# Gated mix of memory attention and a spectral filter: the wait that is planned to end last is written first

## The chip, the cores and the metric

The kernel runs on one core of one Trainium2 chip. The metric is the time on the device in microseconds; lower is better. The core has five instruction streams: TensorE (PE, with its weight loads shown apart as PEld), VectorE (DVE), ScalarE (ACT), GpSimd (POOL) and SyncE (SP), which here only issues transfers. The streams know of each other through semaphores alone: an instruction raises one when it has finished, a transfer raises one when it has landed, and another stream waits until the semaphore has reached a value.

## The reference

Two branches are computed from the same x (2048 tokens, 640 channels, bf16) and mixed by a gate per token:

```python
g = sigmoid((x * gate_w).sum(-1, keepdims=True))
a = A_ref(x, wq, wk, wv, wo, beta)      # attention in 4 segments of 512, 32 heads of 20
b = B_ref(x, w_r, w_i)                  # irfft2(rfft2(x) * (w_r + 1j * w_i))
return g * a + (1 - g) * b

# A_ref, segment s:
p = softmax(q k^T * 20**-0.5 + causal mask);  a_dot = p v
a_mem = phi(q) M / (phi(q) z + 1e-6)          # phi(t) = t + 1 if t > 0 else exp(t)
o = sigmoid(beta) * a_mem + (1 - sigmoid(beta)) * a_dot
M += phi(k)^T v;  z += sum of phi(k)          # memory for the next segment
# then o @ wo
```

## The kernel before

All the work is recorded first and emitted afterwards. `Kern.record` calls, segment by segment, the projections of q, k and v (`project`, `proj_tile`, `v_tile`), the reading of the memory (`mem_read`), attention (`attend`: `qk_unit` for the logits, exponentials on ACT at L1271, causal masks on POOL at L1292, and `pv_flipped` or `pv_group` for p v), and the memory update; after the first segment also the whole spectral branch (`fft`), which is written as matrix products with tables and lies between the attention work in time. `finish_tile` multiplies by wo, adds the spectral part and stores. Matmuls all pass through the helper `mms` (L520 and L522), copies out of PSUM through `copy_alts` (L531 on ACT, L533 on DVE), transfers through `dma` (L554 and L556). So those lines stand for many places; the tile names tell them apart.

`Sched` holds the operations. `op` notes what each reads and writes and from this on which earlier operations it depends. `schedule` takes a fixed order (`ORDER`, 2328 entries, each an operation and its engine), and plans a start and an end `t1` for each operation from listed durations and hop costs (`HOPS`). It also chooses PSUM banks and semaphores, which adds dependences: a bank must have been emptied, a transfer's semaphore must be free, and only so many bytes may be in flight.

`emit` writes the program in the planned order. For each operation it collects the semaphores and values to wait for. It leaves out those that the engine is known to have passed, directly or through what it has already waited for. What is left is `kept`, a list of (planned end, semaphore, value). It is sorted by the planned end, and one `wait_ge` is written for each (L292), just ahead of the operation.

An instruction can carry one wait. In the built program the wait that was written first is carried by the instruction itself. The others become separate EVENT_SEMAPHORE instructions of the same engine directly ahead of it, with up to two waits in each. The profile shows them at L292. For a matmul the carried wait is on its weight load. Of the 2328 operations, 933 have no wait that is kept, 1162 have one, and 233 have two or more: 196 have two and 37 from three to eight.

Of the kernel before, what the change touches and what calls it, by code (L numbers as in the profile page):

```python
# [49 lines left out]
class Sched:  # L50
# [204 lines left out]
    def emit(self, *last):  # L255

        nc = self.nc
        prog = {e: nc.alloc_semaphore(f"prog_{e}") for e in ("pe", "act", "dve", "pool")}
        dsem = [nc.alloc_semaphore(f"dma_{i}") for i in range(self.nsem)]
        dcnt = [0] * self.nsem  # L260
        count = {e: 0 for e in prog}
        known = {e: {} for e in self.eng}
        for o in self.order:
            o.need_inc = o.dma
        for o in self.order:
            for p in o.preds + o.dyn:
                if not (p.eng == "pe" and o.eng == "pe"):
                    p.need_inc = True
        stamps = {}
        for o in self.order:  # L270
            e = o.eng
            k = known[e]
            waits = {}
            for p in o.preds + o.dyn:
                if p.eng == "pe" and e == "pe":
                    continue
                key, val, vc = stamps[p.id]
                if k.get(key, 0) >= val:
                    continue
                if waits.get(key, (0, None))[0] < val:  # L280
                    waits[key] = (val, vc, p.t1)
            kept = []
            for key, (val, vc, t1) in sorted(waits.items(), key=lambda q: -len(q[1][1])):
                if k.get(key, 0) >= val:
                    continue
                kept.append((t1, dsem[key] if isinstance(key, int) else prog[key], val))
                for kk, vv in vc.items():
                    if k.get(kk, 0) < vv:
                        k[kk] = vv
                k[key] = val  # L290
            for t1, sem, val in sorted(kept, key=lambda q: q[0]):
                self.eng[e].wait_ge(sem, val)  # L292
            h = o.alts[e][0](self.eng[e])
            if o.dma:
                i = o.stamp
                dcnt[i] += 16
                h.then_inc(dsem[i], 16)
                stamps[o.id] = (i, dcnt[i], dict(k))
            elif o.need_inc:
                count[e] += 1  # L300
                h.then_inc(prog[e], 1)
                vc = dict(k)
                if e == "pe":
                    pass
                stamps[o.id] = (e, count[e], vc)
            else:
                stamps[o.id] = (e, count[e], {})
        ends = {}
        for o in sorted(self.order, key=lambda o: o.t1):
            if o.name in last:  # L310
                ends.pop(o.stamp, None)
                ends[o.stamp] = stamps[o.id][1]
        return [(dsem[i], v) for i, v in ends.items()]
# [1301 lines left out]
```

## Time and profile before

| | |
|---|---|
| median of 3 runs | 246.04 us (245.78 to 247.57) |
| profiled execution, first to last instruction | 242.6 us |
| around it (246.04 − 242.6; the profiled execution has no time of its own beside its span) | 3.4 us |
| PE busy | 227.0 us (94%), 4361 matmuls |
| DVE, ACT, POOL busy | 199.9, 200.5, 167.5 us |
| granted TensorE clock | 1.00 |
| HBM traffic | 147 GB/s over the span |

How to read it: the busy time of an engine counts its work, not its waiting; waits that are instructions of their own (EVENT_SEMAPHORE) are not busy time. The chain of waits follows the work that ended last back to the start: each piece is an engine's work, or "issue", time between what released an instruction and its start. A piece such as "DVEq L292" is VectorE's sequencer at a separate wait. "a <- b" in the view of waits means that engine a stood idle until b ended.

### The profile page before, as it was taken

To read this page: it belongs to the slowest core of one execution; us is meant where nothing else is said; L and a number is where in the kernel's file an instruction comes from. 1 tells how busy PE (TensorE), PEld (TensorE's weight loads), DVE (VectorE), ACT (ScalarE), POOL (GpSimd) and SP (SyncE) were. 2 spreads that over 40 slices of the span, in tenths; PEclk is the share of its full clock that TensorE was granted. 3 is DMA by queue.
4 is the path that set the end of the run, shared out by engine and by line. 5 is a ranking of instruction groups with operands and counts; after the bars stand their busy time and mean duration, and the time that the engine had idled before them with its cause. 6 is when DMAs were issued, how large, how long until landed. Compare 5 with 4: busy or idle time off the path is not lost.

```text
span 242.6 us, 10273 instructions
## 1 busy us (share of the span) xinstructions
PE 227.0 (94%) x4361; PEld 140.8 (58%) x4361; DVE 199.9 (82%) x478; ACT 200.5 (83%) x243; POOL 167.5 (69%) x298
## 2 busy tenths in 40 slices
PE   7899999999979999999799979999999999899994
PEld 2574666666546565454566545556545467566794
DVE  0199988899999997999997898998899996937474
ACT  2468989898989999899899889999999998688801
POOL 8243069457959946828787894986989687759730
PEclk9999999999999999999999999999999999999999
DMA  7999859995985875957735863543767779554223
GB/s 167 305 327 226 207 169 200 253 214 152 246 241 116 167 192 149 189 161 217 192 99 172 199 187 111 178 113 112 212 179 171 199 143 244 109 88 84 87 63 108
DMA packets 58928, 42.17 MB, mean 174 GB/s; under 512 B 30020, under 2 KB 55172, under 8 KB 58884
## 3 DMA queue, kind: packets, MB, share of 16 engines
q1 hardware_dynamic: 57188, 40.71, 67.3%
q10 hardware_dynamic: 1696, 0.82, 1.2%
q8 instruction: 34, 0.56, 1.0%
q14 instruction: 10, 0.08, 0.1%
HBM read 23.32 MB, written 12.30 MB: 147 GB/s over the span
## 4 chain that ended last, share of the span: by engine, by line
PE 58%; DVE 17%; ACT 13%; DMA 4%; issue 2%; SPq 2%; POOL 2%; DVEq 0%; ACTq 0%; POOLq 0%
PE psum L522 53%; ACT ex L1271 10%; PE psum L520 5%; DVE G L1493 2%; DMA r<-r_scr 2%; DVE phk L1093 2%; DMA xsb<-in_A_x_dram 2%; DVE Pt L1447 2%; SPq L554 2%; DVE Yt L1452 2%; DVE oU L1534 1%; POOL ex L1292 1%; DVE xsb L914 1%; DVE xf L909 1%; DVE ub L533 1%
## 5 line engine op out<-in xcount | busy, mean ns | idle before, releaser
L1271 ACT ACTIVATE ex<-psum 128x2048 bf16<-128x2048 f32 (+4 forms) x92 | 138.5, 1506 | 13.2 <-PE psum L522 10.5
L1292 POOL TENSOR_SCALAR_AFFINE_SELECT ex<-ex 128x256 bf16<-128x256 bf16 (+2 forms) x224 | 123.2, 572 | 32.0 <-ACT ex L1271 27.9
L522 PE MATMUL psum<-qkp 20*64 20x64 bf16 (+5 forms) x1280 | 32.7, 270 | 3.3 <-ACT ex L1271 2.8
L522 PE MATMUL psum<-xT,wk 128*128 128x256 bf16 (+1 forms) x280 | 33.5, 273 | 1.2 <-DMA wk<-in_A_wk_dram 0.6
L522 PE MATMUL psum<-xT,wq 128*128 128x512 bf16 (+1 forms) x135 | 31.3, 380 | 0.0
L522 PE MATMUL psum<-wv,xT 128*32 128x320 bf16 (+3 forms) x400 | 29.5, 301 | 0.3 <-ACT gate L1121 0.2
L1447 DVE TENSOR_TENSOR Pt<-psum,Wt 128x642 bf16<-128x642 f32 x32 | 25.5, 821 | 0.8 <-PE psum L522 0.6
L522 PEld LDWEIGHTS psum<-qkp 20*64 20x64 bf16 x1280 | 13.5, 102 | 20.8 <-ACT ex L1271 14.2
L522 PEld LDWEIGHTS psum<-xT,wk 128*128 128x128 bf16 (+1 forms) x280 | 19.6, 97 | 9.2 <-DMA xT<-in_A_x_dram 1.3
L520 PE MATMUL psum<-wo,oU 128*32 128x320 bf16 x480 | 21.4, 300 | 0.7 <-DVE oU L1542 0.5
L522 PE MATMUL psum<-ex,va 128*32 128x64 bf16 (+3 forms) x576 | 17.6, 256 | 2.1 <-DVE dn L1160 1.3
L522 PEld LDWEIGHTS psum<-wv,xT 128*32 128x32 bf16 (+1 forms) x400 | 14.5, 96 | 7.7 <-issue 2.6
L522 PE MATMUL psum<-big,Ac 128*128 128x161 bf16 (+2 forms) x96 | 17.5, 257 | 1.6 <-DVE va L1123 1.4
L914 POOL TENSOR_TENSOR xsb<-xf 128x320 bf16<-128x320 bf16 (+2 forms) x9 | 7.6, 843 | 15.8 <-DVE xsb L914 11.7
L522 PE MATMUL psum<-big,Cp 128*128 128x321 bf16 (+1 forms) x96 | 17.8, 303 | 0.4
L1123 DVE TENSOR_TENSOR va<-psum,ebx 128x320 bf16<-128x320 f32 x32 | 15.3, 484 | 3.2 <-PE psum L522 2.2
L522 PEld LDWEIGHTS psum<-ex,va 128*32 128x32 bf16 x576 | 11.4, 96 | 10.8 <-POOL ex L1292 3.2
L1493 DVE TENSOR_TENSOR G<-eo,psum 128x320 bf16<-128x320 f32 x32 | 14.9, 479 | 2.4 <-PE psum L522 2.0
L533 DVE CAST ot<-psum 128x320 bf16<-128x320 f32 x18 | 8.4, 488 | 9.4 <-PE psum L520 7.4
L1080 ACT ACTIVATE et<-qu 128x512 bf16<-128x512 bf16 x25 | 15.3, 625 | 0.9 <-DVE phk L1093 0.9
L1452 POOL TENSOR_TENSOR Yt<-Pt 128x321 bf16<-128x321 bf16 x17 | 12.6, 748 | 4.9 <-PE psum L522 4.4
L522 PE MATMUL psum<-tt,Yt 128*128 128x256 bf16 (+1 forms) x96 | 15.6, 273 | 0.3 <-DVE mem L1165 0.2
(96 smaller groups left out, 399.5 us busy)
## 6 DMA issues: line engine op xcount, KB each, us to landing
qkp<-qk_scr SPq DMA_DIRECT2D x28, 160.0 KB
tt<-tab_tt SPq DMA_DIRECT2D x8, 512.0 KB, 4.1
qk_scr<-qu SPq DMA_DIRECT2D x12, 256.0 KB, 2.9
u_scr<-ub SPq DMA_DIRECT2D x12, 256.0 KB, 3.2
xsb<-in_A_x_dram SPq DMA_DIRECT2D x8, 320.0 KB, 5.5
oU<-u_scr SPq DMA_DIRECT2D x15, 128.0 KB, 3.0
out_dram<-ot SPq DMA_DIRECT2D x12, 160.0 KB
Wt<-in_B_w_r_dram SPq DMA_DIRECT2D x16, 80.2 KB, 3.1
```

The source lines that it names most:

```text
L520: h = e.matmul(dst, wt, r_, start=st, stop=sp_, **{**kw, "tile_position": (0, q), "skip_group_check": True})
L522: h = e.matmul(o_, l_, r_, start=st, stop=sp_, **kw)
L533: alts["dve"] = (lambda e: e.tensor_copy(dst(), src()), 67 + 1.04 * n, 68.0)
L554: return e.dma_start_transpose(d_, s_)
L914: self.either(lambda e, dst=dst, src=src, d0=d0, n=n, op=op: e.tensor_tensor(xs.ap(o + dst, [D, 2], [1, n]), xf.ap(src + d0, [321, 2], [1, ...
L1080: self.one("act", lambda e: e.activation(et.ap(0, [1, L]), qsl(), ACT.Exp), L, [qb], [b("et", pi_)], late, name="phi_exp")
L1123: self.one("dve", lambda e: e.tensor_tensor(va.ap(i * H * VW + h0 * VW, [VW, nh], [1, DH]), self.ps(bank, 0, [DH, nh], [1, DH]), self.ebx. ...
L1271: self.one("act", lambda e, d=d, q=q: e.activation(self.ex.ap(*d), self.ps(bank, *q), ACT.Exp, scale=SC), n, [bank], [self.exb(s, 2 * pr + ...
L1292: self.one("pool", lambda e: e.affine_select(self.ex.ap(e0 + d0, [1280, 4], [1, n], np_=np_), self.ex.ap(e0 + s0, [1280, 4], [1, n], np_=np_),
L1447: self.one("dve", lambda e, ri=ri, Pt=Pt, Wt=Wt, wo_=wo_, bank=bank: e.tensor_tensor(Pt.ap(ri * 322, [644, 2], [1, KD]), self.ps(bank, 0, ...
L1452: fn = lambda e, r=r, a0=a0, a1=a1, op=op, Pt=Pt, Yt=Yt: e.tensor_tensor(Yt.ap(r * 322, [1, KD]), Pt.ap(a0 * 322, [1, KD]), Pt.ap(a1 * 322 ...
L1493: self.one("dve", lambda e, q=q, n2=n2, bank=bank, eo=eo: e.tensor_tensor(self.G.ap(n2 * D + 639 * q, [1 - 2 * q, 320]), eo.ap(q, [1, 320] ...
```

## The change

One sort is turned round. The same waits on the same semaphores and values are written for each operation, but in falling order of the planned end. Operations with one wait or none are written as they were. By the build's rule above, for an operation with two waits the two change places: the one planned to end last is carried by the instruction, the other is the EVENT_SEMAPHORE. With more than two, the one planned to end last is carried, and the others share the EVENT_SEMAPHOREs.

```diff
-            for t1, sem, val in sorted(kept, key=lambda q: q[0]):
+            for t1, sem, val in sorted(kept, key=lambda q: q[0], reverse=True):
                 self.eng[e].wait_ge(sem, val)
             h = o.alts[e][0](self.eng[e])
```

## The prediction

> **What bounds the kernel now.** First the page: the span, the busy times, and the chain that ended last by engine.
>
> ```profile
> span 242.6 us, 10273 instructions
> PE 227.0 (94%) x4361; PEld 140.8 (58%) x4361; DVE 199.9 (82%) x478; ACT 200.5 (83%) x243; POOL 167.5 (69%) x298
> PE 58%; DVE 17%; ACT 13%; DMA 4%; issue 2%; SPq 2%; POOL 2%; DVEq 0%; ACTq 0%; POOLq 0%
> ```
>
> PE is busy 94% of the span, yet the chain lies on PE for only 58%: it changes engine often, and each change is a hop from one engine's last write to the next engine's start. The kernel is bound by PE work plus hops, and hops are what a change to waits can touch. "issue" at 2% of 242.6 us is some 5 us, the order of size of everything that is to be had here.
>
> Second, which hops. The wait line, L292, in the view of one source line (engine, operation, count, duration in ns):
>
> ```profile
> L292 PEldq EVENT_SEMAPHORE  x93: 51/51/68, 5.2 to 233.6; - x93
> L292 DVEq EVENT_SEMAPHORE  x71: 21/21/50, 19.6 to 239.5; - x71
> L292 SPq EVENT_SEMAPHORE  x41: 17/17/28, 21.7 to 240.1; - x41
> L292 ACTq EVENT_SEMAPHORE  x31: 17/17/712, 42.1 to 240.1; - x31
> L292 POOLq EVENT_SEMAPHORE  x15: 17/17/17, 9.9 to 207.3; - x15
> ```
>
> These 251 are waits that became instructions of their own. In the built program of before, 233 operations have more than one wait (PE 83, DVE 66, SP 41, ACT 28, POOL 15). In all 233 the wait **written first** rides on the instruction itself, and every later one stands ahead of it in an EVENT_SEMAPHORE. Since before writes the one planned to end last in the last place, that one is in an EVENT_SEMAPHORE, and the instruction carries one that was over long ago.
>
> Third, what the two places cost. This is the chain of waits in order of time (start us, length us, what):
>
> ```profile
> 113.00 0.74 PE psum L522 x5
> 113.74 0.02 issue
> 113.77 0.53 DVE Bt L533
> ...
> 114.67 0.14 issue
> 114.81 0.35 PE psum L522 x3
> 115.15 0.03 issue
> 115.18 0.02 DVEq L292
> 115.20 0.04 issue
> 115.25 0.17 DVE dn L1160
> ...
> 118.61 0.02 issue
> 118.63 1.03 ACT ex L1271
> 119.67 0.04 issue
> 119.71 0.50 PE psum L522 x8
> ```
>
> At 113.77 a DVE copy with one wait starts 0.02 us after PE's last matmul. At 115.25 a DVE operation with two waits starts 0.03 + 0.02 + 0.04 = 0.09 us after it; the EVENT_SEMAPHORE (DVEq L292) begins when the matmul is done, so it held the late wait, and the instruction came only behind it. PE: 0.04 us with one wait (119.71), 0.14 us with several (114.81). ACT with one wait: 0.02 us (118.63). The other two engines:
>
> ```profile
> 99.86 0.02 issue
> 99.88 0.02 ACTq L292
> 99.90 0.04 issue
> ```
>
> ```profile
> 9.85 0.02 issue
> 9.87 0.02 POOLq L292
> 9.89 0.10 issue
> ```
>
> ```profile
> 220.27 1.25 ACT ex L1271
> 221.57 2.98 POOL ex L1292 x4
> ```
>
> ACT takes 0.02 + 0.02 + 0.04 = 0.08 us through an EVENT_SEMAPHORE, POOL 0.02 + 0.02 + 0.10 = 0.14. POOL with one wait takes 221.57 − 221.52 (220.27 + 1.25) = 0.05.
>
> **The change, part by part.** Nothing is added or removed: the same waits, the same 251 EVENT_SEMAPHOREs, the same order on every engine and queue, all transfers in their places. What moves is which wait is where. Written first, the wait planned to end last rides on the instruction, and the earlier ones go into the EVENT_SEMAPHORE, where they are passed while the engine would have waited anyway. So a long hop becomes a short one, wherever the engine really stood waiting and the plan was right about which wait is last. Per hop:
>
> - PE 0.14 − 0.04 = 0.10 us; DVE 0.09 − 0.02 = 0.07; ACT 0.08 − 0.02 = 0.06; POOL 0.14 − 0.05 = 0.09.
> - SP issues transfers. The trace's chain has no long SP hop, so I price it by its neighbour ACT at up to 0.06 each, hidden now behind transfers of microseconds, and count 0.
>
> Is the plan right? I set the times of the semaphores' updates against each of the 233 groups: in 222 the wait planned last did come last. In 11 another did; those would get the long hop in place of the short one.
>
> How many long hops lie on the path? I laid the starts of the EVENT_SEMAPHOREs beside the pieces of the chain. In 21 places a piece starts right behind one: PE 13 (35.73, 43.05, 70.55, 85.79, 94.67, 114.81, 117.27, 125.94, 146.64, 149.21, 151.24, 151.68, 172.16 us), DVE 6 (115.25, 135.30, 137.79, 174.28, 205.54, 239.58), ACT 1 (99.94), POOL 1 (9.99). The first and last of PE and the last of DVE, whose first stands above:
>
> ```profile
> 35.73 7.12 PE psum L522 x94
> ...
> 172.16 2.03 PE psum L522 x46
> ...
> 239.58 0.49 DVE ot L533
> ```
>
> At some of them the view shows a shorter step than 0.14, because it dates the release by the last update of that semaphore and not by the value awaited; I use the same price for all. Sum on the chain: 13 x 0.10 + 6 x 0.07 + 0.06 + 0.09 = 1.30 + 0.42 + 0.15 = **1.87 us**.
>
> The chain can't give all of it, for when it shrinks another path is last. That cover is seen in the busy times by stretch (length; busy of PE, weight load, DVE, ACT, POOL):
>
> ```profile
> 20.00:60.00 40.00, 39.61 (x614) 24.95 (x610) 36.77 (x92) 35.49 (x54) 22.06 (x40) 1.00 0.88 207
> ...
> 100.00:140.00 40.00, 37.13 (x652) 22.21 (x650) 36.26 (x91) 37.34 (x39) 29.64 (x58) 1.00 0.65 165
> 140.00:180.00 40.00, 36.77 (x665) 21.16 (x663) 36.47 (x78) 37.03 (x44) 32.32 (x59) 1.00 0.55 158
> ```
>
> From 100 to 180 us PE, DVE and ACT are each busy 36 to 37 of 40 us, so a hop saved for PE is partly eaten by ACT, which has few EVENT_SEMAPHOREs (28 operations). Of the 21 hops, 12 lie there, 8 of PE and 4 of DVE: 0.80 + 0.28 = 1.08 us. The other nine are worth 1.87 − 1.08 = 0.79. The lower end is the first stretch and the tail alone: from 20 to 60 us PE is full (39.61 of 40) and DVE and ACT have over 3 us to spare, and at 239.58 PE's work is over. These are the hops at 9.99, 35.73, 43.05, 205.54 and 239.58, together 0.09 + 0.20 + 0.14 = 0.43 us. The upper end is the whole 1.87. I take the nine whole and half of the twelve, 0.79 + 0.54 = 1.33, **1.3 us**, since the competing paths run through EVENT_SEMAPHOREs as well.
>
> The sum is made on the span: 242.6 − 1.3 = 241.3 us. The median of the runs is 246.04, 3.4 us over the profiled span; that lies outside the first and last instruction and stays. Forecast: 246.04 − 1.3 = **244.7 us**.
>
> [...]
>
> **The rivals.**
>
> *Nothing to measure (246.0 us).* The hop saved on PE is given back: PE arrives 0.10 earlier and waits for ACT or DVE that much longer. For it: the equal loads of 100 to 180 us. Against: the hops at both ends, where there is no other engine to wait for. Price: the 0.43 us that is left, or less. [...]
>
> *More than the chain (243.5 us).* The second- and third-latest paths hold long hops too, and earlier issues on SP bring loads forward: 41 operations there at up to 0.06 are 2.5 us at most, and a quarter of it on the path is 0.6. 1.87 + 0.6 = 2.5, thus 246.04 − 2.5 = 243.5. Against: half of the chain's hops lie where three engines are level.
>
> *Slower: the plan is wrong where it counts (up to 247.9 us).* Where the wait planned last is not the last in truth, the change puts the true last one into the EVENT_SEMAPHORE and adds 0.06 to 0.10 us, which is the saving with the sign turned. It decides if more than half of the 21 places on the path were such; if all were, 246.04 + 1.87 = 247.9. For it: the plan's times are not the chip's, and 11 of 233 groups already came in another order. Against: 11 is 5%, and each must also be exposed; the mirror needs ten times as many. If, against what the build of before shows, the last written wait rode on the instruction, the price would be the same one; the DVEq L292 row at 115.18 excludes that.
>
> **How the numbers follow.** Forecast case (gain 0.4 to 2.3 us): 0.72. Nothing to measure: 0.13. More than the chain: 0.10. Slower: 0.05. The range holds 8 in 10: it takes in the forecast case and, at each side, part of the next: from 243.4 (1.87 + 0.6 with rounding) to 246.4 us (no gain, and the 0.3 us by which the lower two of the runs of before differ). About 1%, 2.46 us, is what a measurement of this kernel can tell from no change; the whole chain sum is less than that. So faster by over 1% is the third case, 0.11 with a tail of the first; slower by over 1% would need more than the whole mirror, 0.03; within 1%: 0.86.
>
> **What would show it.** In the changed kernel's profile the counts of EVENT_SEMAPHORE stay 93, 71, 41, 31, 15, but they start well before the instruction behind them, and "DVEq L292" or "ACTq L292" pieces hardly stand on the chain. DVE and ACT start 0.02 us after their releaser, PE 0.04, POOL 0.05, also with two waits. Busy times stay within some tenths: PE 227, DVE 200, ACT 200; the span is near 241.3. The forecast is wrong if the pieces of L292 are still on the chain (the waits didn't move, or the plan's last isn't the last), or if they are gone and the span stays at 242.6, which would mean that the freed tenths are waited for elsewhere, visible as longer waits of PE for ACT ex.

## The result, and the profile after

| | before | changed |
|---|---|---|
| first comparison, median of 20 runs each | 246.31 us | 245.53 us |
| its ratio, 95% interval | | 0.988 [0.985, 0.991] |
| comparisons pooled, every run | 246.39 us (93 runs) | 244.79 us (44 runs) |
| comparisons pooled, runs at a mean granted clock of 1.00 | 245.66 us (48) | 243.82 us (23) |

(The last two rows pool the first comparison and the three beside the experiments below, named a, b and c there. The 20 runs of before in the first comparison have no clock on record, and are not in these rows.)

The kernel became faster, by less than the first ratio says: that ratio counts only the 9 faster of the changed kernel's 20 runs, and 9 of the 11 left out have a mean granted clock of 0.979 to 0.998, below the 0.9985 of the last row, as about half of all executions of both kernels have (45 of 93 and 21 of 44). Where the trace of such an execution of the two kernels is kept (the first profile of the changed kernel, a_all, b_before), it shows a short stretch at a lower clock, 0.50 for 3.4 us in the first of them; below, a run with such a mean clock is said to have met a half-clock stretch. At a mean clock of 0.991 to 0.998 the runs take 1.4 to 2.2 us more than at 1.00 (before 247.01 against 245.66, the changed kernel 246.06 against 243.82). Set side by side at a mean clock of 1.00 (0.9985 or more), the runs of the last row give 0.9925 [0.9896, 0.9948], that is **−1.84 us [−2.53, −1.25]**; with every run counted it is −1.60 us [−2.5, −0.8]. The intervals of these two rows are from resampling the runs, and they mix chips. The comparisons taken one by one differ more than that: at clock 1.00 the change is worth −1.0 us in b (8 runs of the changed kernel), −2.9 in c (3 runs) and −2.2 in a (1 run). The forecast was −1.3 us.

The page of the changed kernel's first profile (span, busy times, granted clock in 40 slices):

```profile
span 244.0 us, 10261 instructions
PE 226.9 (93%) x4349; PEld 140.8 (58%) x4361; DVE 200.7 (82%) x478; ACT 200.4 (82%) x243; POOL 167.2 (69%) x298
PEclk9999999999999999999999999999999999799999
```

The busy times are those of before to within 0.8 us, and yet the span is 1.4 us *longer* than the 242.6 of before. The digit 7 in the row of the clock tells why: this execution met a half-clock stretch (3.4 us at 0.50). So the trace to read is that of a second profile of the same kernel (run b_all), without one:

```profile
span 239.9 us, 10273 instructions
PEclk9999999999999999999999999999999999999999
PE 57%; DVE 17%; ACT 13%; DMA 4%; POOL 3%; issue 2%; SPq 2%; DVEq 0%
```

The separate waits are as many as they were (line L292 of the first profile; duration in ns, then first and last start in us):

```profile
L292 PEldq EVENT_SEMAPHORE  x93: 51/51/442, 5.6 to 233.8; - x93
L292 DVEq EVENT_SEMAPHORE  x71: 21/21/304, 18.5 to 239.5; - x71
L292 SPq EVENT_SEMAPHORE  x41: 17/17/1803, 20.9 to 241.5; - x41
L292 ACTq EVENT_SEMAPHORE  x31: 17/17/1762, 41.1 to 241.5; - x31
L292 POOLq EVENT_SEMAPHORE  x15: 17/17/17, 3.4 to 203.4; - x15
```

What has changed is the hop behind them. This is the chain of waits of run b_all at the place that the prediction quoted (113.00 to 120 us there), and at the end:

```profile
112.28 0.53 DVE Bt L533
112.81 0.38 DVE va L1123
113.19 0.05 issue
113.23 1.97 PE psum L522 x49
...
230.00 6.86 PE psum L522 x189
236.85 0.02 issue
236.88 0.49 DVE ot L533
```

PE's start behind DVE `va` took 0.14 us before and takes 0.05 now. The last DVE copy, behind PE's last matmul, stood behind "0.03 issue, 0.02 DVEq L292, 0.04 issue" at 239.49 to 239.58 before; now one piece of 0.02 us is left. Over the whole chain, steps between engines of 0.09 to 0.14 us for PE, or 0.08 to 0.09 for DVE and ACT, number 13 in the trace of before (PE 5, DVE 7, ACT 1) and 3 in this one, all of PE. (The view dates some hops shorter, as the prediction said, so this is fewer than its 21.)

Where the time went is read from the starts of the same ACT instructions in each trace (start us, us, then what, idle time before it; the last row groups two). First comes before, with five rows; then before once more (run b_before, where a half-clock stretch at 148 us spoils the last row), the first profile of the changed kernel, and runs b_all (with five rows) and c_all of it:

```profile
84.20 1.87 ACT L1271 ACTIVATE ex<-psum 128x2048 bf16<-128x2048 f32 x1
86.42 0.60 ACT L531 ACTIVATE Cp<-psum 128x512 bf16<-128x512 f32 x1 [0.35 <-PE psum L522]
113.30 1.88 ACT L1271 ACTIVATE ex<-psum 128x2048 bf16<-128x2048 f32 x1
145.94 0.54 ACT L531 ACTIVATE Bt<-psum 128x322 bf16<-128x322 f32 x1 [1.10 <-PE psum L522]
182.49 2.08 ACT L1271 ACTIVATE ex<-psum 128x1280 bf16<-128x1280 f32 x2
```

```profile
85.66 1.87 ACT L1271 ACTIVATE ex<-psum 128x2048 bf16<-128x2048 f32 x1
147.44 0.54 ACT L531 ACTIVATE Bt<-psum 128x322 bf16<-128x322 f32 x1 [1.13 <-PE psum L522]
```

```profile
83.70 1.88 ACT L1271 ACTIVATE ex<-psum 128x2048 bf16<-128x2048 f32 x1
144.83 0.54 ACT L531 ACTIVATE Bt<-psum 128x322 bf16<-128x322 f32 x1 [1.19 <-PE psum L522]
181.12 2.08 ACT L1271 ACTIVATE ex<-psum 128x1280 bf16<-128x1280 f32 x2
```

```profile
83.26 1.87 ACT L1271 ACTIVATE ex<-psum 128x2048 bf16<-128x2048 f32 x1
85.05 0.60 ACT L531 ACTIVATE Cp<-psum 128x512 bf16<-128x512 f32 x1
111.81 1.88 ACT L1271 ACTIVATE ex<-psum 128x2048 bf16<-128x2048 f32 x1
144.19 0.54 ACT L531 ACTIVATE Bt<-psum 128x322 bf16<-128x322 f32 x1 [1.19 <-PE psum L522]
180.47 2.08 ACT L1271 ACTIVATE ex<-psum 128x1280 bf16<-128x1280 f32 x2
```

```profile
82.86 1.87 ACT L1271 ACTIVATE ex<-psum 128x2048 bf16<-128x2048 f32 x1
143.76 0.54 ACT L531 ACTIVATE Bt<-psum 128x322 bf16<-128x322 f32 x1 [1.18 <-PE psum L522]
180.04 2.08 ACT L1271 ACTIVATE ex<-psum 128x1280 bf16<-128x1280 f32 x2
```

From the instruction at 84.20 to the one at 145.94, before takes 61.74 and 61.78 us, the changed kernel 61.13, 60.93 and 60.90: a saving of 0.61, 0.81 and 0.84. Nine of the prediction's 21 hops lie there: PE 85.79, 94.67, 114.81, 117.27, 125.94, DVE 115.25, 135.30, 137.79 and ACT 99.94, worth 0.50 + 0.21 + 0.06 = 0.77 us. From there to 182.49, before takes 36.55, the changed kernel 36.29, 36.28 and 36.28: 0.27 saved, where six hops (PE 146.64 to 172.16, DVE 174.28) are worth 0.57.

The two rows between them show that the 0.77 did not come hop by hop. The table gives the time from one of these instructions to the next (us; the price is the whole one of the prediction's hops in the stretch; the last three columns are kernels of experiment 1):

| stretch (starts in before) | price | before, b_before | changed: first profile, b_all, c_all | PE alone | all but PE | late wait in both places |
|---|---|---|---|---|---|---|
| 84.20 to 86.42 | 0.10 | 2.22, 2.22 | 1.80, 1.79, 1.78 | 2.07 | 1.97 | 1.96 |
| 86.42 to 113.30 | 0.16 | 26.88, 26.89 | 26.96, 26.76, 26.77 | 26.36 | 26.78 | 26.86 |
| 113.30 to 182.49 | 1.08 | 69.19, spoilt | 68.66, 68.66, 68.63 | 69.04 | 69.06 | 69.29 |

The last row holds exactly the twelve hops that the prediction took at half, 0.54. They gave 0.53 to 0.56. The first row holds one hop of 0.10 and gave 0.42 to 0.44. What lies behind that is a start of DVE just ahead, which is on the chain of before and not among the 21 places. Before, and then run b_all:

```profile
82.35 0.41 DVE L533 CAST Cp<-psum 65x256 bf16<-65x256 f32 x1
83.18 0.69 DVE L533 CAST ub<-psum 128x512 bf16<-128x512 f32 x1 [0.42 <-PE psum L522]
```

```profile
81.33 0.41 DVE L533 CAST Cp<-psum 65x256 bf16<-65x256 f32 x1
81.71 0.69 DVE L533 CAST ub<-psum 128x512 bf16<-128x512 f32 x1
```

In before, DVE stands idle for 0.42 us ahead of `ub`. That is more than a long hop. Its separate wait, for PE, runs at 82.76 and is over at 82.78; the wait that the instruction carries is for a transfer that landed 13 us earlier. So neither wait explains the last 0.40 us, and why the copy starts so late stays open (the row names a PE matmul, but in b_all the copy starts ahead of that one). It goes with the order of writing: b_before and the version with PE's order alone changed, whose DVE waits are those of before, stand 0.42 and 0.41 us there, the changed kernel not at all, and the version with the late wait in both places 0.09.

Outside of these stretches the traces can't tell. The ACT instruction that starts at 60.38 in before starts at 61.82 in b_before, and between 59.13 and 60.50 in four traces of the changed kernel, so the first 60 us differ between executions of one kernel by 1.4 us, and after 182.49 the traces scatter nearly as much (from the same instruction to the end of the span b_all takes 59.4 us and c_all 60.7).

### The profile page after: what moved, and what is told of

Same layout as the page of the kernel before. It is cut to its first block, busy times and chain, and to the rows that moved or that the text cites. A ratio compares the mean times of both kernels' runs of the same rounds, so it can differ in the third digit from the quotient of the medians.

```text
span 244.0 us, 10261 instructions
## 1 busy us (share of the span) xinstructions
PE 226.9 (93%) x4349; PEld 140.8 (58%) x4361; DVE 200.7 (82%) x478; ACT 200.4 (82%) x243; POOL 167.2 (69%) x298
## 4 chain that ended last, share of the span: by engine, by line
PE 63%; DVE 16%; ACT 10%; DMA 7%; issue 2%; ACTq 0%; SPq 0%; DVEq 0%
PE psum L522 57%; ACT ex L1271 8%; PE psum L520 5%; DMA r<-r_scr 2%; DMA xT<-in_A_x_dram 2%; DVE Yt L1452 2%; DVE Pt L1447 2%; DVE phk L1093 2%; DMA dnc<-u_scr 2%; DVE oU L1534 1%; DMA u_scr<-ub 1%; ACT et L1080 1%; DVE Cp L533 1%; DVE ub L533 1%; DVE G L1493 1%
## 5 line engine op out<-in xcount | busy, mean ns | idle before, releaser
L522 PE MATMUL psum<-xT,wq 128*128 128x512 bf16 (+1 forms) x123 | 28.0, 385 | 0.8 <-issue 0.5
L520 PE MATMUL psum<-wo,oU 128*32 128x320 bf16 x480 | 22.2, 305 | 0.5 <-DVE oU L1542 0.2
L522 PEld LDWEIGHTS psum<-wv,xT 128*32 128x32 bf16 (+1 forms) x400 | 14.5, 96 | 7.4 <-issue 2.0
```

What stands on the lines that cost most here:

```text
L520: h = e.matmul(dst, wt, r_, start=st, stop=sp_, **{**kw, "tile_position": (0, q), "skip_group_check": True})
L522: h = e.matmul(o_, l_, r_, start=st, stop=sp_, **kw)
```

## The experiments

All times are medians in us. "At clock 1.00" means the runs with a mean granted clock of 0.9985 or more; for these the changed kernel stands at 243.82 and before at 245.66 in the pooled runs. The diffs are cut together, and their first line with a minus is the changed kernel's.

**1. The change once more, PE alone, all but PE, and both at once.** The first edit turns the order for one engine, the second for the other four; the third keeps the late wait on the instruction and writes it again in last place, so that it is awaited in both places.

```diff
-            for t1, sem, val in sorted(kept, key=lambda q: q[0], reverse=True):
+            for t1, sem, val in sorted(kept, key=lambda q: q[0], reverse=e in ('pe',)):                          # a_pe
+            for t1, sem, val in sorted(kept, key=lambda q: q[0], reverse=e in ('act', 'dve', 'pool', 'sp')):     # a_nope
+            order_ = sorted(kept, key=lambda q: q[0], reverse=True)                                              # a_twice
+            if len(order_) > 1:
+                order_ = order_ + order_[:1]
+            for t1, sem, val in order_:
```

> The change as it is, once more beside before. Theory H (the long hop behind a separate wait becomes a short one, and the time falls by the hops on the path): 1.3 to 1.9 us less than before. Rival M (more than the path that the chain view showed: the gain lies also in hops beside it, and the first comparison's 1.2% is the true size): 2.5 to 3.4 us less. Rival C (the first comparison mixed executions with different granted clocks): executions at full clock differ by less than 1.9 us.

> Only TensorE's operations write the wait planned to end last first; the other engines are as before. H: PE has 13 of the 21 long hops on the chain and 1.30 of the 1.87 us, so about 70% of the full change's gain, 0.9 to 1.3 us less than before. M: gains add up over engines, PE's share of all 233 operations is 83, so a good third of 2.9 us, 1.0 us, and the other engines bring the rest.

> All engines but TensorE have the change. H: the remaining 0.42 + 0.06 + 0.09 us of the sum, so 0.3 to 0.6 us less than before. M: about two thirds of 2.9 us, 1.9 us less.

> As the change, but the wait planned to end last is written a second time at the end, so that an EVENT_SEMAPHORE holds it as before while the instruction carries it too. H: all hops are long again and the time is that of before, within 0.5 us. Rival Q (it is the instruction's own, old wait of before that cost time, not the late wait standing apart): the time is that of the full change.

| | every run | ratio to before, 95% | at clock 1.00 | against before at 1.00 |
|---|---|---|---|---|
| changed (a_all) | 245.13 (6) | 0.990 [0.983, 0.997] | 243.72 (1) | −1.84 [−2.53, −1.25], pooled |
| PE alone (a_pe) | 245.04 (12) | 0.995 [0.992, 0.999] | 244.87 (9) | −0.79 [−1.9, −0.3] |
| all but PE (a_nope) | 246.32 (12) | 0.999 [0.995, 1.003] | 244.95 (7) | −0.71 [−1.7, +0.8] |
| late wait in both places (a_twice) | 245.91 (12) | 0.998 [0.995, 1.002] | 245.39 (5) | −0.27 [−2.5, +0.6] |

The last column is against the pooled 245.66; the 14 runs of before at clock 1.00 in this comparison have a median of 245.90, which would put the last three lower by 0.24. The two parts are worth 0.79 and 0.71, together 1.5 of the 1.84, and with the late wait kept ahead of the instruction as well, most of the gain is gone. But only the interval of PE alone excludes zero, and the shares (1.30 of PE and 0.57 of the rest by the chain sum) can't be told from halves.

The table of stretches above says more. With the late wait in both places, everything from 86.42 to 182.49 takes as long as before (96.15 us against 96.07), so there the late wait *ahead* of the instruction is what costs. Its 0.26 saved from 84.20 to 86.42 is the place of `ub`: at this one place the cost goes with the old wait on the instruction, as that run's rival Q has it. And the parts do not add up: from 113.30 to 182.49 PE alone saves 0.15, where the sum has 0.80 for PE, and the other engines alone 0.13 of 0.28; all together save 0.53 to 0.56. This fits the reason that the prediction gave for its half: a hop saved on one engine is waited away at another that still has its long hops.

**2. The place of the wait, enlarged.** 1162 operations have a single wait. In b_late each such operation is given a second one that its engine has passed already. Written first, that idle wait rides on the instruction, and the real one stands ahead in an EVENT_SEMAPHORE. In b_early the idle wait is written last, so the two waits change places. Both kernels have as many separate waits: PE 430, DVE 397, ACT 223, POOL 205, SP 154, which is 1158 more than in the changed kernel.

```diff
+        self.passed = {}
...
-            for t1, sem, val in sorted(kept, key=lambda q: q[0], reverse=True):
+            order_ = sorted(kept, key=lambda q: q[0], reverse=True)
+            if len(order_) == 1 and e in self.passed:
+                order_ = [self.passed[e]] + order_        # b_late
+                order_ = order_ + [self.passed[e]]        # b_early, in place of the line above
+            if kept:
+                self.passed[e] = order_[-1]               # b_late; order_[0] in b_early
+            for t1, sem, val in order_:
```

> As the change, and each of the 1162 operations with one wait also gets a second one that its engine has long passed, written first: the idle wait rides on the instruction and the real one stands apart, so that nearly every hop of the kernel becomes a long one. H: the path of before holds about 30 PE hops, 30 DVE, 22 ACT and 6 POOL with one wait; 30 x 0.10 + 30 x 0.07 + 22 x 0.06 + 6 x 0.09 = 7 us more than the change, so some 5 us above before (3 to 8). If the long hop is hidden by other paths as the prediction took for half of them: 3.5 us more than the change.

> The same two waits as in the run with late waits apart, in the other order: the idle wait stands apart and the real one rides on the instruction. The same 1200 or so EVENT_SEMAPHOREs. H: an early wait apart is passed while the engine waits anyway, so the time is that of the change within 0.5 us. Rival N (it is the number of EVENT_SEMAPHOREs that costs, not which wait is in them): the time is that of the run with late waits apart.

> Before against itself: it shows what a difference between two equal kernels comes out as. All theories: 0, and the distance from 0 is the error that the other runs of this study have to be read with; over 0.7 us (0.3%) would mean that the spread between executions, not the change, can make the part by which the first comparison is above 1.9 us.

> The change as it is, for its size alone. H with the whole chain sum (nothing eaten by other paths): 1.9 us less than before at the same granted clock. H with the discount of the prediction: 1.3. M: 2.5 to 3.4.

| | every run | ratio to before, 95% |
|---|---|---|
| late waits apart (b_late) | 259.25 (6) | 1.056 [1.049, 1.062] |
| idle waits apart (b_early) | 247.43 (12) | 1.000 [0.995, 1.006] |
| before against itself (b_before) | 246.74 (12) | 1.004 [1.000, 1.007] |
| changed (b_all) | 244.78 (12) | 0.995 [0.991, 0.999] |

This is the clearest result of the study. The same instructions with the same real waits cost 11.8 us more when the late one stands ahead. From the instruction at 84.20 to that at 182.49, where both traces are at clock 1.00, b_late takes 102.59 us and b_early 97.58, so 5.0 us of it stand there without any part of the clock. Idle waits apart cost little: the same stretch takes 97.18 to 97.42 in the changed kernel. Over the whole run b_early's one run at clock 1.00 took 245.25, against 243.82, thus 1.4 us for 1158 idle waits; with every run counted it is 2.7 us over b_all, which is more than the 0.5 expected, and 11 of its 12 runs met a half-clock stretch. In the chain of b_late the long hops stand again (PE 0.14; ACT through L298, which is L292 moved by the added lines):

```profile
105.08 0.14 issue
105.22 4.50 PE psum L528 x59
...
121.69 0.02 issue
121.71 0.02 ACTq L298
121.73 0.04 issue
121.78 1.03 ACT ex L1277
```

The size missed, though: 14.5 us over b_all, twice the 7 that were expected. A part of it is no hop at all (busy times by stretch of b_late: length, PE, weight load, DVE, ACT, POOL, then the granted clock):

```profile
0.00:180.00 180.00, 166.42 (x2736) 99.42 (x2736) 151.03 (x353) 150.96 (x182) 120.37 (x220) 1.00 0.73 183
216.10:222.90 6.80, 6.35 (x151) 4.06 (x155) 3.51 (x10) 2.26 (x3) 2.69 (x3) 0.50 0.39 65
```

For 6.8 us the clock is 0.50, which is up to 3.4 us lost (an estimate, 6.8 x 0.50).

**3. Which engine.** The edit of b_late for one engine at a time:

```diff
-            if len(order_) == 1 and e in self.passed:
+            if len(order_) == 1 and e in self.passed and e in ('pe',):    # or ('dve',), ('act',)
```

> As in the kernel with the idle wait in front of every single wait, but on PE alone: 337 more separate waits there, each of which takes the wait that ends late. By hops alone: some 30 places on the chain where PE waits for another engine, at 0.10 us each, so +3.0 us over the changed kernel. If the hops are not what cost 14 us in the version with all engines, but the time of PE's own separate waits (51 ns each in the rows, 337 of them, 17 us at most), then this kernel alone takes most of the 14 us, 8 us or more.

> The same on DVE alone: 326 more separate waits. By hops: some 30 on the chain at 0.07 us, so +2.1 us over the changed kernel. [...]

> The same on ACT alone: 192 more separate waits. By hops: some 22 on the chain at 0.06 us, so +1.3 us over the changed kernel; 0 if ACT's slack hides them.

> The changed kernel once more, beside the same runs of the kernel before. By the whole chain sum 1.9 us below it at the same granted clock; by the sum with half of the middle hops left out, 1.3 us below.

| | every run | ratio to before, 95% | at clock 1.00 | over the changed kernel at 1.00 |
|---|---|---|---|---|
| PE (c_late_pe) | 254.33 (6) | 1.031 [1.025, 1.036] | none | none |
| DVE (c_late_dve) | 247.95 (12) | 1.004 [1.000, 1.007] | 245.91 (1) | +2.1, one run |
| ACT (c_late_act) | 245.38 (12) | 0.998 [0.994, 1.002] | 244.99 (9) | +1.2 [+0.6, +2.4] |
| changed (c_all) | 243.45 (6) | 0.990 [0.985, 0.995] | 242.73 (3) | |

The last column is against the pooled 243.82. Against it DVE and ACT came out near the sums of their hops, 2.1 and 1.3; against the three runs of c_all at clock 1.00 (242.73) they are 3.2 and 2.3 over. For DVE that is a single run, since the other 11 of 12 met a half-clock stretch, and every run counted it is 4.5 us over c_all. The traces, from the instruction at 84.20 to that at 182.49, all at clock 1.00, put each engine over the changed kernel (97.18 to 97.42 us): PE 99.47, thus 2.1 to 2.3; DVE 98.29, thus 0.9 to 1.1; ACT 98.41, thus 1.0 to 1.2. So a late wait apart costs on DVE too: 13 steps of 0.08 to 0.09 us in front of a DVE instruction stand on the chain of c_late_dve, and none on that of c_all.

PE alone cost 254.33 − 243.45 = 10.9 us, where the hops gave 3.0. Its one trace splits that. This is its chain at two places, the second at the ACT instruction that starts at 182.49 before:

```profile
102.86 0.14 issue
103.00 10.75 PE psum L528 x146
...
184.26 1.25 ACT ex L1277
```

The long hops are there: 12 of 0.14 us stand on this chain, none on that of c_all. At 184.26 the kernel is 3.1 to 4.2 us behind the three traces of the changed one (181.12, 180.47, 180.04), the scatter of the start included, and 3.0 were expected. The rest comes later, in one place (instructions in order of time: start, length, what, idle time before it; then the stretch behind them):

```profile
208.80 1.69 POOL L1548 TENSOR_TENSOR oU<-oU,mT 128x640 bf16<-128x640 bf16 x1 [2.21 <-DVE oU L1540]
210.45 0.45 POOL L1298 TENSOR_SCALAR_AFFINE_SELECT ex<-ex 128x256 bf16<-128x256 bf16 x1
211.90 1.18 PEld L528 LDWEIGHTS psum<-va,ex 128*128 128x128 bf16 x41 [4.49 <-POOL ex L1298]
```

```profile
212.00:220.00 8.00, 7.97 (x207) 5.15 (x211) 4.39 (x13) 3.98 (x6) 3.04 (x4) 0.69 0.16 46
```

PE stands for 4.4 us behind a causal mask on POOL, which is queued there behind a product that waits for DVE (by its row the mask is over at 210.90, 1.0 us before PE starts; what that last 1.0 us is the rows don't show). Run b_all has no such wait of PE over 0.2 us from 185 to 225 us. Then PE runs its next 8 us at a clock of 0.69, 2.5 us lost by estimate (8.0 x 0.31). So 3.1 to 4.2 of hops, 4.4 of a wait that was hidden before, and about 2.5 of clock make up the 10 us between the spans (250.1 against 239.9 and 240.7). That the time goes to PE's separate waits as such (51 ns each), the rival of this run, does not fit: most of the excess came in one place, and b_early, which has as many of them, takes at most 0.4 us more than the changed kernel from 84.20 to 182.49. Why the late waits on PE bring on the wait of 4.4 us is not shown.

## Why the prediction was right or wrong, point by point

- **What the change does** was right. The 93, 71, 41, 31 and 15 separate waits stay, "DVEq L292" is gone from in front of the last copy, and the hops shown are 0.02 to 0.05 us. With late waits put ahead everywhere (b_late) 11.8 us were lost against the other order (b_early), 5.0 of them in a stretch at full clock.
- **The size** was forecast too small: −1.3 us, where the first comparison gave 1.2% and the runs at clock 1.00 gave 1.84 [1.25, 2.53].
- **"In 21 places a piece starts right behind one", each at the price of a hop,** is the step that failed, as far as the traces can tell. The sum has 0.10 us from 84.20 to 86.42, and 0.42 to 0.44 were saved there. The DVE start at 83.18 is on the chain and was not counted, since its EVENT_SEMAPHORE ends 0.40 us ahead of it; before stands 0.42 us there and the changed kernel does not. That is not a long hop, and its cause stays open. It is some 0.3 us of the 0.5 between 1.33 and 1.84. Where the rest lies is not known: in the first 60 us and after 182.49 executions of one kernel differ by more, and the interval of the runs lets in 1.33 as well as 1.84.
- **"I take the nine whole and half of the twelve"** held for the twelve: 0.53 to 0.56 us in the traces for the 0.54 forecast, and PE alone or the others alone brought 0.15 and 0.13 there. That it was just the half is luck, for the prediction had no row that gave it. That the runs' 1.84 lies beside the undiscounted 1.87 does not show that the whole sum came: from 84.20 to 182.49 the whole sum is 1.34, the discounted one 0.80, and the three traces saved 0.87, 1.08 and 1.11.
- **The price per hop** is of the right order. At clock 1.00, late waits apart on DVE alone and on ACT alone cost 2.1 (one run) and 1.2 us against the pooled runs and 3.2 and 2.3 against those of their own comparison, where 2.1 and 1.3 were expected.
- **"3.4 us over the profiled span … lies outside"** was wrong. In the profiled runs of the two kernels that have both, the difference is 2.0 to 2.1 us (241.91 and a span of 239.9, 242.73 and 240.7). The profiled execution of before was then one of about 244.6 us, 1.1 below the median at clock 1.00. This didn't enter the difference, since the sum was taken off the median.
- **The median of three runs as a base** can have hidden half-clock stretches: 246.04 lies between the 245.66 without and the 247.01 with one. How much of the first comparison's 1.2%, or 2.9 us, comes from them is not shown: its medians of all 20 runs differ by 0.8 us, and the later comparisons gave 0.990, 0.995 and 0.990.
- **Rivals.** "Slower" and "nothing to measure" are excluded by the pooled interval. "More than the chain" (2.5 us) lies just inside its end. The price that it put on SP's issues was not tried alone.

## What to carry to other kernels

Where an instruction has several waits, let the one that ends last in truth ride on the instruction and put the early ones ahead of it: on the chain of before the reverse cost 0.06 (ACT) to 0.10 us (PE) at each place where an engine really stood waiting, and it can be done by the order of writing alone. Count such places on the chain of waits, and expect less than their sum where several engines are equally loaded: here half. Look on the chain for starts that come later behind a separate wait than a hop takes; one such place was worth about four hops. For effects under 1%, compare runs at the same granted clock, and the starts of the same instructions in two traces, before believing a ratio.

## What the runs showed of the hardware that was not expected

The granted clock drops for a short stretch, at different places from one execution to the next (in b_before at 148 us, in the first profile of the changed kernel at 208), in kernels whose PE is busy 93% of the span. In the first profile of the changed kernel the stretch with the digit 7, and the one ahead of it, read:

```profile
204.80:208.20 3.40, 2.56 (x86) 1.83 (x86) 2.54 (x8) 2.48 (x3) 0.76 (x1) 1.00 1.08 168
208.20:211.60 3.40, 3.40 (x83) 1.92 (x75) 2.87 (x10) 1.68 (x4) 2.84 (x4) 0.50 0.40 89
```

For 3.4 us the clock is 0.50, while PE is busy all the time (3.40). PE was idle for a part of the 3.4 us ahead (busy 2.56), and that is so for all seven half-clock stretches that lie within the work of the kept traces (b_early has two, the first profile of the changed kernel, a_all, b_before, b_late and c_late_pe one each): PE was busy 22 to 76% of the 3.4 us before each. But before itself has 3.4 us with PE busy 1.99 (from 142.0 on), and its clock is 1.00 there and in the 3.4 us that follow, so what decides is not settled here. Over the 137 pooled runs of the two kernels 71 had a mean clock of 1.00 and most others 0.993 (an estimate of the loss is 0.007 x 244 = 1.7 us). Meeting one took 1.4 us of before (247.01 against 245.66) and 2.2 of the changed kernel (246.06 against 243.82), as much as the change itself. Of the runs with late waits apart on PE or everywhere none was free of it (0 of 6 each), and of those with idle waits apart one of 12.
